# Transposing P in two row tiles of 64 queries, both heads in one step, into two PSUM banks

## The chip, the core and the metric

The kernel runs on one core of a Trainium2 chip. The metric is device time in microseconds (us) of one execution. Engines are named as in the profile: PE is TensorE (PEld its weight loads), DVE VectorE, ACT ScalarE, POOL GpSimd, SP the engine that issues most DMAs.

## The reference, cut to what is computed

```python
def _attn_ref(q, k, v, w1, b1, w2):          # B, H, S, D = 2, 8, 576, 64
    scores = scale * np.matmul(q, k.transpose(0, 1, 3, 2))
    ...
    x = (psi_rel / psi_i)[..., None]
    h = np.maximum(x @ w1 + b1, 0.0)
    bias = h @ w2
    scores = scores + bias.transpose(2, 0, 1)[None, :, :, :]
    scores = scores - np.max(scores, axis=-1, keepdims=True)
    attn = np.exp(scores)
    attn = attn / (np.sum(attn, axis=-1, keepdims=True) + 1e-09)
    return np.matmul(attn, v).astype(np.float32)
...
    x = np.ascontiguousarray(attn_out.transpose(0, 2, 1, 3)).reshape(B * S, H * D)
    x = _moe_ref(x=x, **moe_kwargs)
    return _moe2_ref(x=x, **moe2_kwargs)
```

Attention over 576 positions with a small learned bias for each pair of positions; then a mixture of four experts and a second feed-forward layer, both plain matrix products with elementwise work between them. Only the attention part is touched.

## The kernel before, in words

The attention part comes first and takes about the first 194 us of the span; the two feed-forward parts follow and are not touched. Attention works on pairs of heads: `n` = 0 to 7 is a batch and a head pair, and each `n` has nine score tiles (`g` = 9n to 9n+8): four chunks `c` of 128 queries for each of the two heads `h`, and a last tile (`c` = 4) with the remaining 64 queries of both heads side by side.

For each score tile the work runs like this. `scores` (L670) multiplies q by k into a PSUM tile `big`; `biased` (L684, DVE) adds the bias and finds the row maximum; `exps` (L692, ACT) writes the exponentials P and their sums; `norm_add`, `norm_recip` (L697, L702, DVE) and `norm` (L712, POOL or DVE) divide. Then P, which has queries on its partitions, must be turned so that keys lie on the partitions: `transp` (L729) turns four blocks of 128 x 128 of one head into one PSUM bank, and `transp_rest` (L742, L745) the 64 keys of each head that are left over. In each such instruction the weights that PE loads are a block of P and what streams through is the unit matrix `ident`. `copies` (L755 on ACT, L757 on DVE) brings the turned blocks from PSUM to the tiles `pt` and `pe`. When half of the queries of `n` are there, `av` (L770) multiplies them by v, and ACT and DVE write the result as `x` (L781, L785). `qk_T` (L627) turns q and k of the next `n`; its weights are 128 x 128 blocks too, with a unit matrix of type fp32r streaming.

PSUM has eight banks here: four for the tag `one`, which `transp`, `transp_rest`, `qk_T` and `av` share, and two tiles `big` of two banks each for the scores.

PE runs in different shapes: `scores`, `transp` and `qk_T` use the full array (128 rows, 128 columns), `av` two column tiles of 64 columns, and the bias products (L479) four column tiles of 32. The order of all instructions in attention is made when the program is built: `schedule` gives each step a duration, an urgency (from the numbers in `CFG`) and the steps it waits for, and `Flow.emit` picks from those that are ready; a change of PE's shape costs the time in `TURN` there, and tables in `PICK` say which engine takes a step. The numbers in `CFG` are the same before and after.

Of the kernel before, what the change touches and what calls it, by code (L numbers as in the profile page):

```python
# [18 lines left out]
B, H, S, D, HID = 2, 8, 576, 64, 32  # L19
# [5 lines left out]
P = 128  # L25
# [3 lines left out]
def f32_of_bits(b):  # L29
# [15 lines left out]
START = dict(PE=6.0, ACT=5.06, DVE=5.06, POOL=6.0, SP=7.5)  # L45
ARRIVES = dict(k=7.5, q=8.5, ident=6.5, ltab=10.0)
PORT = {("DVE", "hid"), ("DVE", "norm"), ("DVE", "low")}
TURN = {(32, 128): .22, (32, 64): .15, (64, 128): .16, (64, 32): .15, (128, 32): .11, (128, 64): .14}
NAMES = dict(D="DVE", A="ACT", P="POOL")
PICK = dict(hid="DDAAAADDDADDDDDDAADDDDDDDDAADDDDDDADDADADADDADADADADAADDDDDDDAADDADAADDD"  # L50
              "AADDADADADADDADDADAAADADDDDDAADADDDADADDDDDAADDAADDADAADDDADDDADDDDDAADD",
# [2 lines left out]
            copy="AADDADDAAADAAADADDDADAAADAADADDAAADDDDADAADDDAAAADAAAAAADAAADDAADDDAADAA",  # L54
            rest="AAAAAAAAAAAAAAAADDAAAAAAADAAAAAAAADDAAAAAAADDAAADAAADAAAAAAAAADAAADAAADA",
            high="PPPAAPPAPPAAAPPP",
            low="PPPPDPPDPDDPPDPP")

LAG = {"PE": .2, "ACT": .16, "DVE": .17, "POOL": .14, "SP": 1.5, "": 0.0, "own": .1, "ownPE": 0.0}
# [18 lines left out]
class Flow:  # L78
# [24 lines left out]
    def earliest(self, o):  # L103
        t = max(self.free[o["eng"]], o["after"])
        if o["port"]:
            t = max(t, self.free["port"])
        for h in o["take"]:
            users = self.caps[h["set"]]
            if len(users) > users[0]:
                end = users[-users[0]]["end"]  # L110
                if end is None:
                    return None
                t = max(t, end + LAG["own"])
        return t
# [58 lines left out]
class Kernel:  # L173
# [470 lines left out]
    def attention(self):  # L644

        nc, early = self.nc, self.early
# [57 lines left out]
        def norm(g, e):  # L704
            n, c, h = where(g)
            eng = nc.vector if e == "DVE" else nc.gpsimd
            ri = rsums[n, c][:, h:h + 1]
            pt = Pt[n, c]
            sl = slice(S * h, S * h + S)
            if c == 4:  # L710
                eng.tensor_scalar(out=pt[:, S:S + 64], in0=pt[:, 512:S], scalar1=ri, scalar2=1.0, op0=ALU.mult, op1=ALU.mult)
            eng.tensor_scalar(out=pt[:, sl], in0=pt[:, sl], scalar1=ri, scalar2=1.0, op0=ALU.mult, op1=ALU.mult)  # L712

        def pt_tiles(n, half):
            if (n, half) not in PT:
                W = (256, 320)[half]
                PT[n, half] = (self.att.tile([P, 4, 2, W], F32, tag=f"pt{half}", bufs=2, name="pt"),
                               self.att.tile([P, W], F32, tag=f"pe{half}", bufs=2, name="pe"))
            return PT[n, half]

        def transp(g):

            n, c, h = where(g)
            main, _ = pt_tiles(n, 0 if c < 2 else 1)
            pt = Pt[n, c]
            o = P * (c % 2) if c < 4 else 256
            ps = self.one().rearrange("p (e i) -> p e i", e=4)
            for e in range(4):
                nc.tensor.transpose(ps[:, e, :], pt[:, 640 * h + e * P:640 * h + e * P + P], self.ident)  # L729
            if c < 4:  # L730
                todo = [(ps, main[:, :, h, o:o + P])]
            else:
                todo = [(ps.rearrange("p e (h q) -> p e h q", h=2), main[:, :, :, 256:320])]
            parts[g] = (todo, [])

        def transp_rest(g):
            n, c, h = where(g)
            _, shared = pt_tiles(n, 0 if c < 2 else 1)
            ps = self.one()
            if c < 4:  # L740
                for i in range(2):
                    nc.tensor.transpose(ps[:, P * i:P * i + P], Pt.pop((n, c - 1 + i))[:, 512:640], self.ident)  # L742
                rest = [(ps[:, 0:256], shared[:, 0:256])]
            else:
                nc.tensor.transpose(ps[:, 0:P], Pt.pop((n, c))[:, 512:640], self.ident)  # L745
                rs = [slice(64 * hh, 64 * hh + 64) for hh in range(2)]
                rest = [(ps[r, r], shared[r, 256:320]) for r in rs]
            parts[g] = (parts[g][0], rest)

        parts = {}  # L750

# [49 lines left out]
        def schedule():  # L801

            def off(kind, n):

                return cfg[kind][min(n, 2) + (n == 7)]

            fl = Flow(cfg["EPS"], cfg["M"], self.behind, **START)
            Top, Sop, Rop, Lop, Lop2, split_op, qk_ops, stk = ({} for _ in range(8))
            biasop = {}
            last_store, made = self.bias_ops(fl, biasop)  # L810
            identr = fl.op("", ARRIVES["ident"], 0, lambda: None)
# [37 lines left out]
            for n in range(8):  # L849
                p_hold = {}  # L850
                for r in range(9):
                    g = 9 * n + r
                    c, h = r // 2, r % 2
                    half = 0 if c < 2 else 1
                    big = fl.hold("big", 2)
                    last = r == 8
                    Sop[g] = fl.op("PE", 1.2 if last else .58, g + off("S", n), lambda g=g: scores(g), qk_ops[n, "k"] + qk_ops[n, "q"] + [biasop[n // 2, c]],
                                   take=[big], free=[stk[n, "k"], stk[n, "q"]] if last else [])
                    ph = fl.hold("P", NPB) if h == 0 else ph
                    Rop[g] = fl.op("DVE", .71, g + off("R", n), lambda g=g: biased(g), [Sop[g], biasop.get((n // 2, c)), Rop[g - 1] if h else None], take=[ph] if h == 0 else [], free=[big])  # L860
# [6 lines left out]
                    for g in ([g] if last else [g - 1, g]):  # L867
                        h = (g - 9 * n) % 2
                        no = fl.pick("norm", g, {"POOL": .88 if last else .72, "DVE": .6 if last else .42}, g + off("N", n), lambda e, g=g: norm(g, e), [ao])
                        one, one2 = fl.hold("one", 4), fl.hold("one", 4)  # L870
                        rest = last or h and c % 2
                        take = [one]
                        if (n, half) not in pt_hold:
                            pt_hold[n, half] = fl.hold("PT", 4)
                            take.append(pt_hold[n, half])
                        to = Top[g] = fl.op("PE", .44, g + off("T", n), lambda g=g: transp(g), [no, Top.get(g - 1)], take=take)
                        Lop[g] = fl.pick("copy", g, {"ACT": .5, "DVE": .6}, g + off("H", n), lambda e, g=g: copies(g, 0, e), [to], free=[one])
                        if h and not rest:
                            ph_even = ph
                        if rest:  # L880
                            to = fl.op("PE", .09 if last else .19, g + off("T", n) + .1, lambda g=g: transp_rest(g), [to], take=[one2],
                                       free=[ph] if last else [ph_even, ph])
                            Lop2[g] = fl.pick("rest", g, {"ACT": .44 if last else .3, "DVE": .3 if last else .33}, g + off("H", n) + .1, lambda e, g=g: copies(g, 1, e), [to], free=[one2])
                    if n % 2 and (h == 1 or last) and n < 7:
                        biasop[n // 2 + 1, c] = fl.op("SP", 1.6 if last else .45, g + off("b", n), lambda n=n, c=c: self.load_bias(n // 2 + 1, c), [Rop[g], last_store if last else None], pipe=.9 if last else 1.85)
                    if r in (3, 8):
                        gs = range(9 * n, 9 * n + 4) if r == 3 else range(9 * n + 4, 9 * n + 9)
                        deps = [raw_op[n, "v"]] + [Lop[x] for x in gs] + [Lop2[x] for x in gs if x in Lop2]
# [452 lines left out]
```

## Time and profile before

| | before |
|---|---|
| median of 3 runs | 784.37 us (784.01 to 786.3) |
| the profiled execution | 784.95 us |
| its span in the profile | 783.2 us |
| PE busy in the span | 764.3 us (98%) |
| DVE, ACT, POOL busy | 638.4, 462.3, 373.1 us |

The span is the profiled part of one execution; 1.8 us lie around it. Busy times of PE include the pipeline's overlap, so a busy PE is not one at its best pace. The chain of work that ended last, which the rows below use, lists pieces that follow one another without a gap: the time of a piece is what it added to the chain.

### The profile page before, as it was taken

How to read it: one execution, taken by the hardware profiler on the slowest of the kernel's cores; microseconds unless marked ns; L12 is line 12 of the kernel's file. 1: busy time of each engine (PE TensorE's matmuls, PEld its weight loads, DVE VectorE, ACT ScalarE, POOL GpSimd, SP SyncE). 2: the span in 40 equal slices, each digit the busy share in tenths (PEclk: the TensorE clock that was granted, in tenths of full speed). 3: DMA queues.
4: the chain of work that ended last, by engine and by line, in shares of the span. 5: the costliest groups of instructions: out<-in, count | busy, mean ns of one | idle time of the engine just before them, and what ended most of it. 6: DMA issues, size and time to landing. Idle time of an engine off the chain costs nothing.

```text
span 783.2 us, 13021 instructions
## 1 busy us (share of the span) xinstructions
PE 764.3 (98%) x4756; PEld 657.3 (84%) x4756; DVE 638.4 (82%) x1139; ACT 462.3 (59%) x892; POOL 373.1 (48%) x361
## 2 busy tenths in 40 slices
PE   6889999999999999999999999999999999999997
PEld 3338888876989989889989889989888989999996
DVE  7998989874788888788888788887679877887775
ACT  7997898783434333333333333333279998887772
POOL 1123544260285553465453365453257777755442
PEclk9999999999999999999999999999999999999999
DMA  6898885730024433444333444332221311000012
GB/s 179 284 296 232 213 212 116 213 101 16 28 80 144 128 112 104 141 148 134 117 112 107 141 145 130 121 113 75 54 82 54 108 54 54 1 1 0 1 41 81
DMA packets 70448, 87.62 MB, mean 112 GB/s; under 512 B 34288, under 2 KB 42736, under 8 KB 70256
## 3 DMA queue, kind: packets, MB, share of 16 engines
q1 hardware_dynamic: 69808, 86.63, 37.1%
q8 instruction: 37, 0.61, 0.3%
q10 hardware_dynamic: 576, 0.16, 0.1%
q14 instruction: 27, 0.22, 0.1%
HBM read 60.15 MB, written 21.61 MB: 104 GB/s over the span
## 4 chain that ended last, share of the span: by engine, by line
PE 77%; DVE 6%; ACT 4%; issue 4%; DMA 4%; POOL 3%; SPq 1%; DVEq 0%; POOLq 0%; ACTq 0%
PE ps_o L945 21%; PE ps_o L1203 13%; PE ps_h L1195 12%; PE ps_y L1037 11%; PE ps_x L1037 8%; PE ps L670 3%; PE ps L770 3%; PE ps L729 3%; DMA rawq<-q 1%; DVE hid L464 1%; ACT P L692 1%; PE ps_x L935 1%; POOL we L344 1%; PE ps L479 1%; PE ps L627 1%
## 5 line engine op out<-in xcount | busy, mean ns | idle before, releaser
L945 PE MATMUL ps_o<-we,hs 128*128 128x512 f32 x810 | 203.4, 392 | 0.0
L945 PEld LDWEIGHTS ps_o<-we,hs 128*128 128x128 f32 x810 | 146.0, 188 | 25.9
L951 DVE SCALAR_TENSOR_TENSOR acc<-ps_o,prob,acc 128x512 f32<-128x512 f32 x135 | 99.8, 744 | 30.0 <-PE ps_o L945 29.9
L344 POOL TENSOR_TENSOR we<-wstg,we 128x512 fp32r<-128x512 f32 x39 | 55.8, 1450 | 129.6 <-ACT we L337 129.6
L1176 POOL TENSOR_TENSOR qq<-qq,ha 128x384 f32<-128x384 f32 x48 | 48.9, 1020 | 74.4 <-ACT qq L1173 70.8
L1203 PE MATMUL ps_o<-wmh,hs 128*128 128x512 f32 x252 | 83.4, 391 | 0.0
L1195 PE MATMUL ps_h<-x,wmh 128*128 128x384 f32 x288 | 73.7, 336 | 0.0
L975 ACT ACTIVATE hs<-ps_x 128x576 fp32r<-128x576 f32 x32 | 20.9, 652 | 80.9 <-DVE ps_x L1049 74.2
L692 ACT ACTIVATE P<-P,nm 128x576 f32<-128x576 f32 x72 | 55.6, 781 | 6.2 <-DVE nm L684 3.9
L684 DVE CUSTOM_DVE_ANT_0 P<-ps,bias 128x576 f32<-128x576 f32 x72 | 53.4, 750 | 6.4 <-PE ps L670 2.7
L712 POOL TENSOR_SCALAR P<-P,ri 128x576 f32<-128x576 f32 x42 | 33.6, 809 | 47.4 <-DVE ri L702 26.8
L1203 PEld LDWEIGHTS ps_o<-wmh,hs 128*128 128x128 f32 x252 | 47.3, 188 | 9.8 <-POOL hs L1187 0.4
L1195 PEld LDWEIGHTS ps_h<-x,wmh 128*128 128x128 f32 x288 | 52.6, 188 | 2.0
L370 POOL TENSOR_TENSOR wu<-wt,wu 128x512 fp32r<-128x512 f32 x28 | 36.2, 1315 | 36.4 <-ACT wu L366 36.4
L1187 POOL TENSOR_TENSOR hs<-pp,hs 128x384 fp32r<-128x384 f32 x48 | 51.8, 1079 | 3.2 <-issue 2.8
L479 PE MATMUL ps<-hid,wm 128*32 128x288 f32 (+17 forms) x352 | 41.0, 495 | 9.8 <-DVE hid L464 6.1
L1182 DVE SCALAR_TENSOR_TENSOR qq<-qq,rr 128x384 f32<-128x384 f32 x48 | 26.6, 553 | 29.3 <-ACT rr L1181 28.2
L670 PE MATMUL ps<-kh,qs 128*128 128x288 f32 x168 | 49.7, 318 | 0.1
L1203 PE MATMUL ps_o<-wml,hs 128*128 128x512 f32 x126 | 49.5, 393 | 0.0
L1037 PEld LDWEIGHTS ps_x<-sums,wu 128*128 128x128 f32 x336 | 47.5, 188 | 2.2
L1037 PEld LDWEIGHTS ps_y<-x,wu 128*128 128x128 f32 x336 | 47.5, 188 | 2.2
L1037 PEld LDWEIGHTS ps_y<-sums,wu 128*128 128x128 f32 x336 | 47.5, 188 | 2.2
(146 smaller groups left out, 1871.1 us busy)
## 6 DMA issues: line engine op xcount, KB each, us to landing
wstg<-moe_w SPq DMA_DIRECT2D x32, 512.0 KB, 3.9
bias_d<-bo SPq DMA_DIRECT2D x32, 295.5 KB, 3.6
bias<-bias_d SPq DMA_DIRECT2D x16, 576.0 KB, 5.2
w<-moe_w_in SPq DMA_DIRECT2D x16, 512.0 KB, 4.2
w<-moe_w_out SPq DMA_DIRECT2D x16, 512.0 KB, 3.8
kl<-kh SPq DMA_DIRECT2D x16, 288.0 KB, 4.7
w_u<-wmag SPq DMA_DIRECT2D x16, 256.0 KB, 2.5
w_d<-wmag SPq DMA_DIRECT2D x16, 256.0 KB, 2.4
```

The costliest lines, as they stand in the source:

```text
L344: eng.tensor_tensor(out=lo[:, sl], in0=stg[:, sl], in1=hi[:, sl].bitcast(F32), op=ALU.subtract)
L479: nc.tensor.matmul(to[32 * q:32 * q + 32, 0:b - a], lhsT=wm, rhs=hs[q][:, a:b], start=True, stop=True)
L670: nc.tensor.matmul(ps[:, half, dst:dst + w], lhsT=lhs, rhs=k[:, src:src + w], start=(i == 0), stop=(i == len(m) - 1))
L684: nc.vector.tensor_tensor_reduce(out=Pt[u][:, S * h:S * h + S].rearrange("p (a b) -> p a b", a=2), in0=ps[:, :, 0:288], in1=self.bias_t[n ...
L692: nc.scalar.activation(out=pt, in_=pt, func=AF.Exp, scale=-1.0, bias=stat.pop(g), accum_out=sums[n, c][:, h:h + 1])
L945: nc.tensor.matmul(ps, lhsT=a, rhs=w[:, f, :], start=(f == i == 0), stop=(f == 1 and i == 2))
L951: nc.vector.scalar_tensor_tensor(out=acc[:, t], in0=ps, scalar=pr, in1=acc[:, t], op0=ALU.mult, op1=ALU.add)
L1037: nc.tensor.matmul(ps[:, half, 0:288], lhsT=wu[:, w, i, k], rhs=x[v][:, k, 288 * half:288 * half + 288], start=(start and k == j == 0), st ...
L1176: nc.gpsimd.tensor_tensor(out=qq, in0=qq, in1=ha, op=ALU.mult)
L1187: nc.gpsimd.tensor_tensor(out=lo, in0=pp, in1=hi.bitcast(F32), op=ALU.subtract)
L1195: nc.tensor.matmul(ps, lhsT=w[:, k, fo:fo + P], rhs=x2_rows(q, v, k), start=(k == i == 0), stop=(k == 3 and i == 2))
L1203: nc.tensor.matmul(ps, lhsT=a[:, P * tt:P * tt + P], rhs=w[:, f % 2, :], start=(f == i == 0), stop=(f == 3 and i == 2))
```

## The change

One step now turns both heads' blocks of a chunk of 128 queries. The 128 x 128 block is split by queries: rows 0 to 63 and rows 64 to 127 of P are each loaded as weights of 64 rows and 128 columns into their own half of the array's rows, 64 columns of the unit matrix stream through each, and each half writes to its own bank of the tag `one`. The step takes two such banks at once, and waits for both heads' `norm`. The rest of two chunks, and the last tile with its rest, are split in the same way. The planner gets durations for the new steps, a shape of PE of its own (`ROWS`), times for turning to it and from it, and two short tables for the added copies. Where 328 blocks were turned by 328 matmuls, there are now 656.

```diff
+ROWS = 65
+TURNED = dict(T=.5, last=.35, rest=.14)
-TURN = {(32, 128): .22, (32, 64): .15, (64, 128): .16, (64, 32): .15, (128, 32): .11, (128, 64): .14}
+TURN = {(128, 65): .15, (65, 128): .2, (65, 32): .15, (32, 65): .2, (64, 65): .15, (65, 64): .15, (32, 128): .22, (32, 64): .15, (64, 128): .16, (64, 32): .15, (128, 32): .11, (128, 64): .14}
...
+        def halves(at, src, *tiles):
+            for r, ps in enumerate(tiles):
+                rows = slice(64 * r, 64 * r + 64)
+                nc.tensor.transpose(ps[:, 64 * at:64 * at + 64], src[rows], self.ident[rows, rows])
+
         def transp(g):
...
-            ps = self.one().rearrange("p (e i) -> p e i", e=4)
+            ps = self.one(), self.one()
+            if c < 4:
+                for e in range(4):
+                    for h in range(2):
+                        halves(2 * e + h, pt[:, 640 * h + e * P:640 * h + e * P + P], *ps)
+                o = P * (c % 2)
+                parts[g] = [[(ps[r].rearrange("p (x i) -> p x i", x=8), main.rearrange("p e h i -> p (e h) i")[:, :, o + 64 * r:o + 64 * r + 64])] for r in range(2)]
+                return
             for e in range(4):
-                nc.tensor.transpose(ps[:, e, :], pt[:, 640 * h + e * P:640 * h + e * P + P], self.ident)
...
+                halves(e, pt[:, e * P:e * P + P], *ps)
+            halves(4, Pt.pop((n, c))[:, 512:640], *ps)
...
-                to = Top[g] = fl.op("PE", .44, g + off("T", n), lambda g=g: transp(g), [no, Top.get(g - 1)], take=take)
...
+                    take = ones = [fl.hold("one", 4) for _ in range(2)]
...
+                    to = Top[g] = fl.op("PE", TURNED["last" if last else "T"], g + off("T", n), lambda g=g: transp(g), norms + [Top.get(g - 1)], take=take, free=[ph] if last else [], mode=(ROWS, ROWS))
```

Two places in PE's order show how the change moves instructions. In these rows `ps<-ident,P` is a turning of P, `ps<-kh,qs` and `ps<-kl,qs` are scores, `ps<-pt,rawv` and `ps<-pe,rawv` are `av`; the numbers are the output's partitions and columns. The first place is late in attention, behind an `av`. Before, four steps of turning (one head's chunk each), one score tile and the rest of two chunks stood like this:

```order
L729 MATMUL ps<-ident,P 128x128 x16
L670 MATMUL ps<-kh,qs 128x288
L670 MATMUL ps<-kl,qs 128x288
L670 MATMUL ps<-kh,qs 128x288
L670 MATMUL ps<-kl,qs 128x288
L742 MATMUL ps<-ident,P 128x128 x2
```

After the change, at the same place, one step of turning (both heads of a chunk) stands between the `av` and the scores:

```order
L779 MATMUL ps<-pe,rawv 64x256 x2
L730 MATMUL ps<-ident,P 128x64 x16
L676 MATMUL ps<-kh,qs 128x288
L676 MATMUL ps<-kl,qs 128x288
```

A run of turnings between score tiles is now a change of PE's shape on either side, where before it was none. The second place is the end of attention. Before, all turnings of the last `n` were done, then three `av` in a row, then the first product of the feed-forward part (`ps<-x,we`, 24 matmuls):

```order
L729 MATMUL ps<-ident,P 128x128 x16
L742 MATMUL ps<-ident,P 128x128 x2
L729 MATMUL ps<-ident,P 128x128 x4
L745 MATMUL ps<-ident,P 128x128
L770 MATMUL ps<-pt,rawv 64x320 x8
L770 MATMUL ps<-pe,rawv 64x320 x2
L770 MATMUL ps<-pt,rawv 64x256 x8
L770 MATMUL ps<-pe,rawv 64x256 x2
```

After the change that product is cut in three pieces, which stand between four runs of turnings, ahead of the last `av`:

```order
L730 MATMUL ps<-ident,P 128x64 x16
L945 MATMUL ps<-x,we 128x288 x6
L730 MATMUL ps<-ident,P 128x64 x16
L945 MATMUL ps<-x,we 128x288 x15
L730 MATMUL ps<-ident,P 128x64 x4
L945 MATMUL ps<-x,we 128x288 x3
L730 MATMUL ps<-ident,P 128x64 x10
L779 MATMUL ps<-pt,rawv 64x320 x8
L779 MATMUL ps<-pe,rawv 64x320 x2
L945 MATMUL ps_x<-x,we 128x288 x24
```

What moved: the product no longer stands behind the last `av`, and each of its pieces is entered from a run of row tiles. Counted over the whole attention part, PE's order before enters the full array 19 times, two column tiles 10 times and four column tiles 9 times; after the change it enters the full array 46 times, row tiles 40 times, two column tiles 15 times and four 9 times.

## Rows read from the trace of the kernel before

**Rows 1.** Busy time in three stretches; in brackets the instructions.

```profile
core 0: us, PE busy (x) PEld busy (x) DVE busy (x) ACT busy (x) POOL busy (x), PEclk, DMA share, GB/s
0.00:60.00 60.00, 48.58 (x405) 22.17 (x409) 54.31 (x145) 54.26 (x113) 10.67 (x19) 1.00 0.82 255
60.00:194.00 134.00, 132.37 (x1088) 108.25 (x1079) 109.58 (x311) 103.78 (x253) 54.84 (x72) 1.00 0.61 158
194.00:783.00 589.00, 583.34 (x3273) 526.90 (x3271) 474.53 (x685) 304.29 (x527) 307.57 (x270) 1.00 0.28 87
```

**Rows 2.** PE's waits behind 195 us: total us, times, longest.

```profile
PE ps_o L945 <- DVE acc L949: 0.6, 1, 0.6
PE ps_x L1229 <- DVE acc L951: 0.5, 1, 0.5
PE ps_x L1229 <- DVE pp L1184: 0.2, 1, 0.2
```

**Rows 3.** The chain that ended last, 128 to 200 us: start, us, what.

```profile
128.90 0.87 PE ps L729 x8
...
178.01 5.00 PE ps L770 x40
183.01 1.90 PE ps L729 x16
184.90 0.22 PE ps L742 x2
...
193.36 3.37 PE ps L935 x24
196.73 3.18 PE ps_x L935 x24
```

**Rows 4.** PE's groups of turnings: count, busy us, mean ns, idle before.

```profile
L729 PE MATMUL ps<-ident,P 128*128 128x128 f32 x288 | 39.9, 276 | 1.2 <-DVE x L785 0.7 <-DVE P L712 0.2
...
L742 PE MATMUL ps<-ident,P 128*128 128x128 f32 x32 | 6.2, 275 | 0.0
...
L745 PE MATMUL ps<-ident,P 128*128 128x128 f32 x8 | 2.2, 276 | 0.0
```

**Rows 5.** The chain again, 94 to 99 us.

```profile
94.23 0.47 PE ps L627 x6
94.69 0.46 PE ps L729 x4
...
98.86 0.47 PE ps L627 x6
```

**Rows 6.** Groups of weight loads, 0 to 200 us: count, busy us, mean ns, idle before.

```profile
L729 PEld LDWEIGHTS ps<-ident,P 128*128 128x128 f32 x288 | 31.8, 141 | 6.6 <-issue 2.0 <-POOL P L712 1.8 <-PE ps L770 1.0
...
L479 PEld LDWEIGHTS ps<-hid,wm 128*32 128x32 f32 x352 | 14.7, 113 | 30.4 <-ACT hid L462 8.0 <-DVE hid L464 6.4 <-POOL wm L443 5.8
L627 PEld LDWEIGHTS ps<-identr,splk 128*128 128x128 f32 x72 | 7.5, 140 | 3.9 <-POOL splk L611 1.8 <-PE ps L479 0.8 <-ACT hid L462 0.6
```

**Rows 7.** DVE's groups of copies and divisions, 0 to 200 us.

```profile
L757 DVE COPY pt<-ps 128x512 f32<-128x512 f32 x30 | 20.0, 683 | 3.0 <-PE ps L729 2.6 <-DMA bias<-bias_d 0.4
L712 DVE TENSOR_SCALAR P<-P,ri 128x576 f32<-128x576 f32 x30 | 17.3, 594 | 0.2
...
L757 DVE COPY pe<-ps 128x256 f32<-128x256 f32 x8 | 3.3, 418 | 0.1
...
L757 DVE COPY pe<-ps 64x64 f32<-64x64 f32 x8 | 1.7, 216 | 0.1
```

**Rows 8.** ACT's groups of copies, 0 to 200 us.

```profile
L755 ACT ACTIVATE pt<-ps 128x512 f32<-128x512 f32 x42 | 23.9, 598 | 3.4 <-PE ps L729 3.3
...
L755 ACT ACTIVATE pe<-ps 128x256 f32<-128x256 f32 x8 | 3.1, 386 | 1.3 <-PE ps L742 1.3
...
L755 ACT ACTIVATE pe<-ps 64x64 f32<-64x64 f32 x8 | 1.7, 216 | 0.0
```

**Rows 9.** POOL's division, 0 to 200 us.

```profile
L712 POOL TENSOR_SCALAR P<-P,ri 128x576 f32<-128x576 f32 x42 | 33.6, 809 | 47.4 <-DVE ri L702 26.8 <-DVE sm L697 6.3 <-ACT kh L635 4.0
```

More of the change, by code (lines that the diff above doesn't have):

```diff
@@ L56 @@
             high="PPPAAPPAPPAAAPPP",
+            copyb="DADADADA",
+            restb="AAAAAAAAAAAAAAAA",
             low="PPPPDPPDPDDPPDPP")
@@ L106, in earliest @@
             t = max(t, self.free["port"])
+        asked = {}
         for h in o["take"]:
-            users = self.caps[h["set"]]
-            if len(users) > users[0]:
-                end = users[-users[0]]["end"]
+            users, k = self.caps[h["set"]], asked.get(h["set"], 0)
+            asked[h["set"]] = k + 1
+            if len(users) + k > users[0]:
+                end = users[k - users[0]]["end"]
                 if end is None:
@@ L719, in pt_tiles @@
             return PT[n, half]
+        def halves(at, src, *tiles):
+            for r, ps in enumerate(tiles):
+                rows = slice(64 * r, 64 * r + 64)
+                nc.tensor.transpose(ps[:, 64 * at:64 * at + 64], src[rows], self.ident[rows, rows])
         def transp(g):
             n, c, h = where(g)
-            main, _ = pt_tiles(n, 0 if c < 2 else 1)
+            main, shared = pt_tiles(n, 0 if c < 2 else 1)
             pt = Pt[n, c]
-            o = P * (c % 2) if c < 4 else 256
-            ps = self.one().rearrange("p (e i) -> p e i", e=4)
-            for e in range(4):
-                nc.tensor.transpose(ps[:, e, :], pt[:, 640 * h + e * P:640 * h + e * P + P], self.ident)
[L730 to L734, printed above, removed]
+            ps = self.one(), self.one()
[6 more added lines that the diff above has]
+                return
+            for e in range(4):
+                halves(e, pt[:, e * P:e * P + P], *ps)
+            halves(4, Pt.pop((n, c))[:, 512:640], *ps)
+            parts[g] = [[(ps[r][:, 0:256].rearrange("p (e i) -> p e i", e=4), main[:, :, r, 256:320]),
+                         (ps[r][64 * r:64 * r + 64, 256:320], shared[64 * r:64 * r + 64, 256:320])] for r in range(2)]
         def transp_rest(g):
@@ L738, in transp_rest @@
             _, shared = pt_tiles(n, 0 if c < 2 else 1)
[L739 to L748, printed above, removed]
+            ps = self.one(), self.one()
+            for i in range(2):
+                halves(i, Pt.pop((n, c - 1 + i))[:, 512:640], *ps)
+            parts[g] += [[(ps[r][:, 0:P].rearrange("p (c i) -> p c i", c=2), shared[:, 0:256].rearrange("p (c r i) -> p c r i", c=2, r=2)[:, :, r])] for r in range(2)]
         parts = {}
@@ L807, in schedule @@
             fl = Flow(cfg["EPS"], cfg["M"], self.behind, **START)
-            Top, Sop, Rop, Lop, Lop2, split_op, qk_ops, stk = ({} for _ in range(8))
+            Top, Sop, Rop, Lop, split_op, qk_ops, stk = ({} for _ in range(7))
             biasop = {}
@@ L866, in schedule @@
                     ao = fl.op("DVE", .11, g + off("A", n), lambda g=g: norm_recip(g), [ao])
[L867 to L875, printed above, removed]
-                        to = Top[g] = fl.op("PE", .44, g + off("T", n), lambda g=g: transp(g), [no, Top.get(g - 1)], take=take)
[L877 to L883, printed above, removed]
@@ new lines, in schedule @@
+                    norms = []
+                    for x in ([g] if last else [g - 1, g]):
+                        norms.append(fl.pick("norm", x, {"POOL": .88 if last else .72, "DVE": .6 if last else .42}, g + off("N", n), lambda e, x=x: norm(x, e), [ao]))
+                    rest = not last and c % 2
+                    take = ones = [fl.hold("one", 4) for _ in range(2)]
+                    if (n, half) not in pt_hold:
+                        pt_hold[n, half] = fl.hold("PT", 4)
+                        take = take + [pt_hold[n, half]]
@@ new lines, in schedule @@
+                    to = Top[g] = fl.op("PE", TURNED["last" if last else "T"], g + off("T", n), lambda g=g: transp(g), norms + [Top.get(g - 1)], take=take, free=[ph] if last else [], mode=(ROWS, ROWS))
+                    Lop[g] = [fl.pick("copyb" if last and r else "copy", n if last and r else g - 1 + r if not last else g, {"ACT": .7, "DVE": .6} if last else {"ACT": .5, "DVE": .6}, g + off("H", n),
+                                      lambda e, g=g, r=r: copies(g, r, e), [to], free=[ones[r]]) for r in range(2)]
@@ new lines, in schedule @@
+                    if c % 2 == 0:
+                        ph_even = ph
+                    if rest:
+                        ones = [fl.hold("one", 4) for _ in range(2)]
+                        to = fl.op("PE", TURNED["rest"], g + off("T", n) + .1, lambda g=g: transp_rest(g), [to], take=ones, free=[ph_even, ph], mode=(ROWS, ROWS))
+                        Lop[g] += [fl.pick("restb" if r else "rest", 2 * n + c // 2 if r else g, {"ACT": .27, "DVE": .25}, g + off("H", n) + .1,
+                                           lambda e, g=g, r=r: copies(g, 2 + r, e), [to], free=[ones[r]]) for r in range(2)]
@@ L887, in schedule @@
                         gs = range(9 * n, 9 * n + 4) if r == 3 else range(9 * n + 4, 9 * n + 9)
-                        deps = [raw_op[n, "v"]] + [Lop[x] for x in gs] + [Lop2[x] for x in gs if x in Lop2]
+                        deps = [raw_op[n, "v"]] + [y for x in gs if x in Lop for y in Lop[x]]
                         one = fl.hold("one", 4)
```

## The prediction, made blind

> **What bounds the kernel now.** I read the busy times by stretch first. From 60 to 194 us, the second part of attention, PE is busy 132.37 of 134 us, DVE 109.58 and ACT 103.78 [rows 1]. In the first 60 us PE is busy 48.58, DVE and ACT 54.31 and 54.26: that stretch is not PE's. Behind 194 us PE is busy again, 583.34 of 589 us, and the list of its waits there has three lines that come to 1.3 us [rows 2]: what attention gains or loses moves the rest by as much. So the question is what the change does to PE between 60 and 194 us, and the chain of waits shows that stretch as PE pieces that follow one another [rows 3]. The granted clock is 1.00 in all three stretches, so no term below is a clock's.
>
> **The price of a turned block now.** Eight blocks behind other full-array work add 0.87 us to the chain, 0.109 each [rows 3]. The 288 of L729, the 32 of L742 and the 8 of L745 are 328 blocks [rows 4]: 328 x 0.109 = 35.8 us of PE time.
>
> **The price after the change.** No row shows row tiles. A block becomes two loads of 64 rows by 128 columns and two streams of 64 columns. Three bounds:
>
> - If the halves run side by side and every load is hidden, only the stream counts, and it is half as long: 0.109 / 2 = 0.0545 a block, 17.9 us in all, 17.9 less than now.
> - If the loads set the pace: `qk_T` loads 128 x 128 weights as well, its loads last 140 ns against 141 for P [rows 6], and six of them add 0.47 us, 0.078 each [rows 5]. Its stream is of type fp32r and quicker than P's, so what holds it at 0.078 is, I take it, the load; with P's stream cut to 0.0545 the load would be the longer one here too. With the loads of the two halves side by side a block takes 0.078: 25.6 us, 10.2 less.
> - If the loads of the two halves go one behind the other, it takes 2 x 0.078 = 0.156: 51.2 us, 15.4 more.
>
> Do loads of different tiles go side by side? Those of the bias products do: 352 loads of 113 ns are 39.8 us, within 14.7 us of busy time [rows 6], 2.7 at a time. These are column tiles with 32 columns each; I take the same for row tiles, and 0.078, since the load keeps its 128 columns and `qk_T` is the nearest row: **-10.2 us**.
>
> **The changes of shape.** This is the part that the diff doesn't show and the order does. Sixteen blocks behind an `av` add 1.90 us [rows 3], 0.156 more than 16 x 0.109: the price of going from column tiles to the full array for a turning. The first product, 24 matmuls behind an `av`, takes 3.37 us against 3.18 for the next 24 [rows 3]: 0.19. PE now enters row tiles 40 times where it never did (40 x 0.156 = 6.2), enters the full array 46 times for 19 (27 x 0.19 = 5.1), and column tiles of 64 fifteen times for ten (5 x 0.156, an estimate, = 0.8): **+12.1 us**. Before, the 70 borders in that order between turnings and scores or `qk_T` were within one shape and cost next to nothing (four blocks behind `qk_T` take 0.46 us, 0.02 over 4 x 0.109 [rows 5]). Row tiles could be entered for less than column tiles: the lower bound is nothing, and that ends at -10.2; the upper one is that of the rows, as I know of none that is dearer. The Trainium skill says, in "TensorEngine Tiling (Array Packing)", Key Properties, that changing the tiling mode, not just the tile, drains the engine. The rows show the price for column tiles; no row shows it for row tiles. Without that rule this term would be nothing and the sum about 9 us better; with it, it stands.
>
> **The copies.** A copy of eight blocks of 64 columns is as long as one of four of 128: 128x512, 0.683 us on DVE, 0.598 on ACT [rows 7, 8]. The last tile's copy is cut in two of 128x256 (like 0.418 and 0.386), and the rest's 16 copies of 128x256 become 32 of 128x128, which lie between the 64x64 (0.216) and the 128x256; I take 0.3. By the order DVE now has 23 long copies for 30 and ACT 37 for 42, with 7 and 9 of 128x256 and 8 and 24 of 128x128 in exchange. DVE: -7 x 0.683 + 7 x 0.418 + 8 x 0.3 - 8 x 0.418 = -2.8 us; ACT: -5 x 0.598 + 9 x 0.386 + 24 x 0.3 - 8 x 0.386 = +4.6 us. ACT has 30 us free in the 134, so this costs nothing by itself; without that cover it would be the 4.6.
>
> **New waits.** A step of turning now waits for both heads' division, where the first head's blocks could go ahead by themselves; a division is 0.594 us on DVE and 0.809 on POOL [rows 7, 9]. And it takes two of the four banks `one` at once, for which `qk_T` and `av` stand too. Behind a waiting turning on PE stand scores, for which DVE waits, and `av`, for which ACT waits. Now the loads of L729 sit idle 6.6 us in all [rows 6]; I bound the new waits between nothing (the planner has 40 runs to fill around) and as much again, 6.6, and take **+1.5**. The move of the first product ahead of the last `av` costs its three entries, counted above; behind the last `av` PE goes on with a product that needs no x of this `n`, so it is not missed as a cover.
>
> **Sum.** -10.2 + 12.1 + 1.5 = +3.4 us. The profiled execution took 784.95 us, 1.8 more than its span, so 788.35; it lies 0.58 above the median of the runs shown, which makes 787.8, and I say 788.
>
> **The rivals.** What 0.3% is here, 2.4 us, is about what a measurement of this kernel can tell from no change.
>
> 1. *The halves overlap fully (faster).* Then a block is 0.0545: -17.9 + 12.1 + 1.5 = -4.3, 780. For it: column tiles do run side by side. Against it: `qk_T` doesn't get below 0.078. It decides at a block of 0.0675 = 0.109 - 13.6 / 328; under 0.060 it is faster by more than 0.3%. The Trainium skill says in "TensorE: Matmul & The Clock Gate", Measured speedup vs the span model, that packed tiles take one matmul's duration and about 4 ns for each further tile. By that a pair would be an estimated 0.0585, -16.6 + 12.1 + 1.5 = -3.0, so 781; it is a figure for matmuls, and says nothing of the loads between them. Chance 0.22, with cheap entries counted in.
> 2. *In between (no change).* The diff's table books 0.5 us for a step of eight blocks, 0.0625 each; the old entry, 0.44 for four, is what the rows give (4 x 0.109). With 32 such steps, 8 last ones at 0.35 and 16 rests at 0.14 turning takes 21.0 us: -14.8 + 12.1 + 1.5 = -1.2, 783. It is a number that the planner plans by and no row. Chance 0.2.
> 3. *Loads one behind the other.* +15.4 + 12.1 + 1.5 = +29, 813. For it: the side-by-side rows are all of column tiles, and none has 128 columns. Chance 0.1.
> 4. *The waits.* Two banks at once starve the others, and the order, made by urgencies that are older than the new steps, leaves PE waiting 6.6 us more instead of 1.5: 793. For it: only four banks, and DVE and ACT busy for 80% of the stretch. Chance 0.13.
>
> **How the numbers follow.** The forecast has 0.35. Its own range goes from 785 (no new wait, a pair at 0.073) to 791. Faster: rival 1 and a little of 2, 0.24. Same: most of 2 and the lower end of the forecast, 0.25. Slower: the rest, 0.51. The range goes from 780, rival 1's time, to 797, which holds rival 4 with some more, and leaves out rival 3 and the better half of 1, about 2 in 10.
>
> **What would show it.** In the changed profile: a run of 16 halves that adds 0.6 to 0.65 us to the chain, with 0.16 on top when it comes from another shape (0.44 means rival 1, 1.25 rival 3); scores behind it that take 0.19 more; the stretch from 60 us to the first product of the feed-forward part longer by some 3 us, with PE still busy in nearly all of it; PE's idle time before turnings near 8 us and not 13. The prediction is wrong if turning into row tiles costs clearly less than 0.15, if a pair takes under 0.065, or if the first 60 us move.

## The result, and the profile after

| | before | after |
|---|---|---|
| median, taken side by side | 785.29 us (784.01 to 786.3) | 790.41 us (790.25 to 790.86) |
| the profiled execution | 784.95 us | 790.39 us |
| its span | 783.2 us | 788.6 us |

The ratio is 1.0067, with an interval from 1.0048 to 1.0086: the change made the kernel slower by about 5 us. The forecast was 788 in a range of 780 to 797, with a chance of 0.51 for slower. What the sum was made of came out quite differently, though, and the profile shows it.

I read the same views in the same order. Busy time in the three stretches of [rows 1], columns as there, of the kernel after:

```profile
0.00:60.00 60.00, 48.66 (x434) 21.84 (x438) 54.57 (x146) 54.77 (x116) 10.65 (x19) 1.00 0.82 256
60.00:194.00 134.00, 128.57 (x1337) 99.45 (x1329) 106.46 (x310) 102.96 (x264) 55.34 (x72) 0.97 0.61 158
194.00:783.00 589.00, 587.29 (x3318) 529.80 (x3317) 474.07 (x685) 306.72 (x535) 307.45 (x270) 1.00 0.27 86
```

In the middle stretch PE is idle for 134 - 128.57 = 5.43 us, where [rows 1] left 134 - 132.37 = 1.63. And the granted clock, 1.00 before, is 0.97 there. Neither stood in my sum in that size. The first stretch is as it was.

The groups of turnings, which answer to [rows 4] and the first row of [rows 6] (count, busy us, mean ns, idle before):

```profile
L730 PE MATMUL ps<-ident,P 64*128 64x64 f32 x656 | 32.1, 232 | 1.2 <-ACT pt L764 0.3 <-ACT pe L764 0.2 <-POOL P L718 0.2
...
L730 PEld LDWEIGHTS ps<-ident,P 64*128 64x128 f32 x656 | 25.3, 140 | 11.3 <-issue 4.7 <-ACT pt L764 1.1 <-DVE P L718 0.8
```

Twice as many loads of the same length (140 ns for 141) are busy for less time than before, 25.3 us for 31.8 of L729 alone. The 656 of 140 ns are 91.8 us, 3.6 at a time; the 288 of 141 ns were 40.6 us, 1.3 at a time.

The chain of waits, from the first `av` behind 60 us to the first products of the feed-forward part (start, us, what); it answers to [rows 3] and [rows 5]:

```profile
60.65 2.36 PE ps L779 x20
...
72.32 8.79 DMA kl<-kh
...
85.10 0.64 PE ps L730 x16
85.74 0.73 PE ps L676 x4
...
87.24 0.60 ACT pt L764
...
88.75 0.77 ACT kh L641 x2
89.51 0.78 ACT qs L641 x2
...
91.15 1.26 PE ps L676 x4
...
92.81 1.26 PE ps L676 x4
...
94.80 2.22 PE ps L676 x8
...
192.53 0.64 PE ps L730 x16
...
198.37 0.38 ACT pt L764
...
198.79 3.28 PE ps L779 x20
202.07 2.98 PE ps_x L945 x21
```

And three rows of the same view of the kernel before, for the comparison:

```profile
61.28 2.31 PE ps L770 x20
...
73.09 0.53 PE ps L670 x4
...
80.76 6.39 DMA rawq<-q
```

Three things are to be seen here. First, a run of 16 halves (eight blocks) takes 0.64 us, entry included. By the ends of its matmuls the two halves of a block end 2 to 7 ns apart, the first block adds 0.206 us and each of the seven others 0.062, so a block is **0.062 us** and the entry 0.206 - 0.062 = 0.144; the four scores behind it take 0.73 where they took 0.53, so the way back is 0.20. (The expectations below still reckon with 0.0586 a block and 0.174 an entry, from the mean of the fifteen steps between the sixteen ends, 29.3 ns. Eight of these steps lie within a block and only seven between blocks, so twice the mean is too little for a block and leaves too much for the entry; the run as a whole is the same.) Secondly, the chain leaves PE, for a transfer of `kl` and for copies on ACT. That alone shows no wait: the chain of the kernel before leaves it too, for a transfer of `rawq`, while PE is busy with other work. Thirdly, from 90.8 us on four scores take 1.26 us and eight 2.22.

What PE did wait for is in the list of its waits from 55 to 203 us (total us, times, longest; the four longest of eight, the others come to 0.9 us):

```profile
PE ps L676 <- DVE nm L690: 1.8, 3, 1.0
PE ps L633 <- POOL splq L617: 1.3, 1, 1.3
PE ps L676 <- DMA kl<-kh: 1.2, 1, 1.2
PE ps L779 <- ACT pt L764: 0.5, 1, 0.5
```

And why scores became slow is in the clock's column of the stretches (us, PE busy, granted clock, DMA share, GB/s):

```profile
78.00:80.00 2.00, 1.56 (x11) 1.00 1.06 261
80.00:82.00 2.00, 0.85 (x6) 1.00 1.05 340
...
90.00:91.00 1.00, 0.89 (x16) 0.89 0.37 83
91.00:92.00 1.00, 1.00 (x7) 0.50 1.23 212
...
96.00:97.00 1.00, 1.00 (x7) 0.50 0.70 161
97.00:98.00 1.00, 1.00 (x9) 0.70 0.61 136
```

From 90.8 to 97.6 us the chip granted 0.50, the lower of its two levels (1.2 instead of 2.4 GHz). The same stretch of the kernel before:

```profile
78.00:80.00 2.00, 2.00 (x18) 1.00 1.02 232
80.00:82.00 2.00, 2.00 (x18) 1.00 1.05 376
```

So PE had waited ahead of the fall, 1.59 of the 4 us from 78 to 82. But the fall came 9 us behind that; from 82 to 87 us PE was busy throughout, and from 87 to 91 us for 3.64 of 4 us. Which of these waits the fall belongs to, this trace doesn't show.

**Where the 5.4 us went.** From that first `av` to the second product, the kernel before took 196.73 - 61.28 = 135.45 us and the one after 202.07 - 60.65 = 141.42: +5.97. The start lies 0.63 earlier, the rest is unchanged to 0.1. I added up, matmul by matmul, what each end adds to the one ahead of it, and set what is above the usual pace of its kind apart: the work of PE fell from 129.3 to 126.6 us (-2.6), its waits rose from 6.2 to 11.8 (+5.6), 4.9 of it before 100 us, and the slow clock cost +3.0. The total is measured; how it splits is an estimate, as it rests on what I took as the usual pace. (The waits in this count are larger than idle time in the table, since the modelled ends of matmuls cover part of them.) So the row tiles did bring time, and waits and the clock took more.

### The profile page after: what moved, and what is told of

The parts are those of the page before. It is cut to its first block, busy times and chain, and to the rows that moved or that the text cites. A ratio compares the mean times of both kernels' runs of the same rounds, so it can differ in the third digit from the quotient of the medians.

```text
span 788.6 us, 13657 instructions
## 1 busy us (share of the span) xinstructions
PE 765.7 (97%) x5084; PEld 651.7 (83%) x5084; DVE 637.0 (81%) x1142; ACT 464.5 (59%) x913; POOL 373.4 (47%) x361
## 4 chain that ended last, share of the span: by engine, by line
PE 78%; DVE 6%; DMA 4%; issue 4%; ACT 3%; POOL 3%; SPq 1%; DVEq 0%; POOLq 0%; ACTq 0%
PE ps_o L955 20%; PE ps_o L1213 12%; PE ps_h L1205 12%; PE ps_y L1047 10%; PE ps_x L1047 8%; PE ps L779 4%; PE ps L676 4%; PE ps L730 2%; DVE hid L470 1%; PE ps_x L945 1%; POOL we L350 1%; DMA kl<-kh 1%; DVE P L690 1%; PE ps L485 1%; PE ps_y L945 1%
## 5 line engine op out<-in xcount | busy, mean ns | idle before, releaser
L485 PE MATMUL ps<-hid,wm 128*32 128x288 f32 (+18 forms) x352 | 41.0, 492 | 9.5 <-DVE hid L470 6.1
```

What stands on the lines that cost most here:

```text
L485: nc.tensor.matmul(to[32 * q:32 * q + 32, 0:b - a], lhsT=wm, rhs=hs[q][:, a:b], start=True, stop=True)
```

## The experiments

Why are there new waits and a slow clock? The step could cost them by itself: it needs both heads' rows and two of four banks. Or it lies in the order: all of attention is set by one list of priorities, and a step with another duration shuffles all that follows. These two stand together as theory A at first; theory B is that the row tiles pull the clock down. Experiments 4 to 8 then tell the two halves of A apart, as theories S (structure) and O (order).

**1. The order of after, without row tiles.** Each block is turned by one matmul on the full array again, head by head into the same two banks; the planner still reckons with row tiles and gives the same order.

```diff
-                for e in range(4):
-                    for h in range(2):
-                        halves(2 * e + h, pt[:, 640 * h + e * P:640 * h + e * P + P], *ps)
+                for h in range(2):
+                    for e in range(4):
+                        nc.tensor.transpose(ps[h][:, P * e:P * e + P], pt[:, 640 * h + e * P:640 * h + e * P + P], self.ident)
```

> The changed kernel with its own order of instructions, but each pair of 64-row halves is one 128 x 128 turning on the full array again (328 matmuls, the same two banks a step). Theory A (the change's PE work is a gain of about 2.6 us; what it loses are new waits of PE that come from the order, +5.6, and a fall of the granted clock after them, +3.0): turning costs 328 x (0.109 - 0.0586) = 16.5 us more and the changes of shape fall away (-13.1), so up to 3.4 us slower than the changed kernel where PE is the limit and nothing where it waits: 790 to 794 us, waits between 60 and 100 us as before, clock at 0.5 again for some us near 90. Theory B (row tiles themselves pull the clock down): clock 1.00 throughout, 787 to 790 us.

Measured: 790.59 us (787.46 to 793.6), 1.0047 (1.0024 to 1.0069) of before. Its rows of the middle stretch and of some microseconds in it, columns as above:

```profile
60.00:194.00 134.00, 128.22 (x1032) 103.60 (x1026) 106.42 (x309) 102.70 (x262) 55.57 (x72) 0.99 0.61 158
```

```profile
81.00:82.00 1.00, 0.00 (x0) 1.00 1.02 336
82.00:83.00 1.00, 0.34 (x3) 1.00 1.09 358
...
84.00:85.00 1.00, 1.00 (x6) 0.50 1.05 321
```

No row tile is left, and yet PE is idle for 5.78 us and the clock falls, right behind idle time. So row tiles are not needed for the clock to fall, and theory B does not hold as the explanation. Whether they make a fall likelier is not shown; all four executions of the changed kernel have a mean clock of 0.995. Here not every execution has the fall: five of the ten, with a mean clock of 0.999 to 1.000, took 787.5 to 789.9 us, and the five with 0.994 to 0.998, the profiled one among them, 791.3 to 793.6. That distance of some 4 us is not the clock's alone: the profiled one has a single fall, of 3.4 us at 0.50, which can cost PE 1.7 us at most. What else differs between the two groups is not shown. The unchanged kernel has such executions as well: beside this run it took 787.29 and 787.37 us at 0.996, and 783.63 to 786.3 at 0.999 to 1.000.

**2. Both heads and two banks on the full array, planned as such.** As in 1, with the planner told so:

```diff
-TURNED = dict(T=.5, last=.35, rest=.14)
+TURNED = dict(T=.88, last=.55, rest=.22)
...
-                    to = Top[g] = fl.op("PE", TURNED["last" if last else "T"], g + off("T", n), lambda g=g: transp(g), norms + [Top.get(g - 1)], take=take, free=[ph] if last else [], mode=(ROWS, ROWS))
+                    to = Top[g] = fl.op("PE", TURNED["last" if last else "T"], g + off("T", n), lambda g=g: transp(g), norms + [Top.get(g - 1)], take=take, free=[ph] if last else [], mode=(128, 128))
```

> The other part of the change alone: both heads in one step with two banks, full-array turning, and the planner told its true durations (0.88, 0.55, 0.22 us) and no change of shape. Theory A (waits come from steps that are twice as long and hold two banks, put in order by urgencies made for the old steps): slower than before without any row tile, 788 to 797 us, with PE's waits between 60 and 194 us of 10 us or more against 6.2. Theory B (the loss is of row tiles: shapes and clock): no slower than before, 784 to 787 us.

Measured: 791.92 us (791.33 to 792.84), 1.0076 (1.0061 to 1.0091), at a clock of 1.000. Its middle stretch:

```profile
60.00:194.00 134.00, 128.19 (x1036) 103.74 (x1028) 105.25 (x307) 101.63 (x260) 54.33 (x72) 1.00 0.62 158
```

PE's idle time there is 134 - 128.19 = 5.81 us. (The 10 us or more of waits that theory A named are in another count, by the ends of the matmuls, which I did not make here.) So with no row tile and no slow clock it is slower than before by some 6 us. That leaves the step's structure or the order.

**3. PE kept busy.** In the changed kernel, of the turning of q and k at `n` = 3 two parts of three are done three times over, so that PE has more to do where it waited.

```diff
-            nc.tensor.transpose(ps[:, P * i:P * i + P], spl[:, c].rearrange("p a d -> p (a d)"), self.identr)
+            for _ in range(3 if n == 3 and part else 1):
+                nc.tensor.transpose(ps[:, P * i:P * i + P], spl[:, c].rearrange("p a d -> p (a d)"), self.identr)
```

> The changed kernel, with twelve of the turnings of q and k of n = 3 done three times over (24 more matmuls of 0.085 us, 2.0 us, that write the same values), in the stretch from 87 to 91 us where PE waits for ACT's copies just before the granted clock falls. Theory A (the fall follows a stretch in which PE has little to do): the clock stays at 1.00, and the time is 3.0 us less and up to 2.0 more than the changed kernel's: 787.4 to 789.4 us. Theory B (row tiles pull the clock down): it falls as before, 790.4 to 792.5 us.

Measured: 791.68 us (789.75 to 793.29), 1.0071 (1.0046 to 1.0095). The clock fell all the same, now from 81.6 to 85.0 us, behind two microseconds in which PE was busy for 0.07 and 0.09. The added work had not filled this gap; the expectation of a clock of 1.00 failed, and the trial settles nothing about the waits.

**4 and 5. The kernel before, in another order.** Nothing of the work is touched; the planner only reckons with another duration for a turning step.

```diff
-                        to = Top[g] = fl.op("PE", .44, g + off("T", n), lambda g=g: transp(g), [no, Top.get(g - 1)], take=take)
+                        to = Top[g] = fl.op("PE", .43, g + off("T", n), lambda g=g: transp(g), [no, Top.get(g - 1)], take=take)
```

> The kernel before, with one number of its planner altered: a turning step of four blocks is put down at .43 us in place of .44. Every instruction stays, with its shape, its banks and its data; only the order that the planner writes out becomes another. Theory O (the order before was one that its priorities had been tuned to, and any change of the steps' costs loses that, so that the change's +5 us lie in the order and not in the row tiles or the two banks): 4 to 9 us slower than before, 789 to 795, with new waits of TensorE before 100 us. Theory S (the structure costs it: a turning step that waits for both heads' rows and takes two banks): no structure is altered here, so within 0.3% of before, 783.5 to 788.5.

> The same with .46 in place of .44: a second order of the same instructions. Theory O: again 4 to 9 us slower than before, 789 to 795, at other waits than with .43. Theory S: within 0.3% of before, 783.5 to 788.5.

Measured: 794.6 us (792.98 to 794.84), 1.0115 (1.0089 to 1.0141) with .43, and 790.9 (789.76 to 793.03), 1.0079 (1.0057 to 1.0101) with .46. Here is the middle stretch with .43, and the list of PE's waits from 55 to 203 us:

```profile
60.00:194.00 134.00, 127.27 (x1030) 104.05 (x1030) 107.17 (x301) 102.26 (x246) 54.61 (x72) 0.99 0.61 158
```

```profile
PE ps L729 <- DVE P L712: 3.8, 2, 2.2
PE ps L670 <- DVE nm L684: 2.6, 2, 1.8
PE ps L479 <- DVE nm L684: 2.4, 1, 2.4
```

With .46 the stretch is:

```profile
60.00:194.00 134.00, 128.41 (x1048) 104.98 (x1039) 107.67 (x307) 101.08 (x248) 55.14 (x72) 1.00 0.60 157
```

Idle time is 6.73 us with .43 and 134 - 128.41 = 5.59 with .46, for 1.63 before. The same instructions, with the same banks and one head at a time, lose as much as the change did, or more. In the trace with .43 the clock falls too, twice for 3.4 us, and up to 3.4 of its 9 us are the clock's; in that with .46 it stays at 1.00. Theory S said nothing would move; it falls as the cause of such waits in general. The order before sits on numbers that fit it, and a hundredth of a microsecond in a planned duration is enough to lose that.

**6 and 7. The change in an order fitted to it.** The changed kernel with other numbers in `CFG` and `PICK`, looked for until the planner's own reckoning of PE's end was back where it stands for the kernel before (its reckoning only chose the candidate; the time is the chip's). One dependence is written out, which the order after happened to keep: the rest of two chunks is turned behind the first chunk's step.

```diff
-            high="PPPAAPPAPPAAAPPP",
+            high='PPPAAPPPPPAPAAPP',
...
-            low="PPPPDPPDPDDPPDPP")
+            low='PPPDDPPDDPPPDDPP')
...
-                        to = fl.op("PE", TURNED["rest"], g + off("T", n) + .1, lambda g=g: transp_rest(g), [to], take=ones, free=[ph_even, ph], mode=(ROWS, ROWS))
+                        to = fl.op("PE", TURNED["rest"], g + off("T", n) + .1, lambda g=g: transp_rest(g), [to, Top[g - 2]], take=ones, free=[ph_even, ph], mode=(ROWS, ROWS))
```

The second kernel of the pair has this order to the letter, and the full array as in 1.

> The changed kernel, with its two row tiles, both heads in one step and two banks, and with other numbers in the two tables that set the order and the engine of each small piece of work (the priorities of each kind of step by head, and which of two engines takes each copy, division and split). Theory O: TensorE's new waits of 5.6 us go again and its 2.6 us less of work stay, so 2 to 5 us below before: 781 to 785. Theory S: the waits come from the step that needs both heads and two banks, so another order helps little: 788 to 792, as the changed kernel. If the clock falls to 0.5 for some us again, up to 3 us come on top with either.

> The order of after_retuned to the letter, but every block turned by one matmul on the full array, 128 x 128, into the same two banks: no row tile is left. By the pace of the changed kernel's turnings (328 blocks, 0.0586 us in place of 0.109: 16.5 us less, against 13.1 us of new entries between shapes) TensorE has about 3.4 us more work than in after_retuned. If the row tiles are a gain by themselves: 2 to 4 us slower than after_retuned. If the entries eat the gain: within 1.5 us of it.

Measured: 781.06 us (779.15 to 782.46), 0.9943 (0.9921 to 0.9966) with row tiles, and 784.0 (782.94 to 785.02), 0.9984 (0.9974 to 0.9993) with the full array, on the same chip, before at 785.22. The middle stretch and two waits of the first, and some of its chain:

```profile
60.00:194.00 134.00, 132.40 (x1417) 103.42 (x1418) 113.46 (x327) 104.92 (x269) 50.72 (x65) 1.00 0.61 157
```

```profile
PE ps L617 <- POOL splq L601: 0.8, 1, 0.8
PE ps L617 <- DVE pt L750: 0.3, 1, 0.3
```

```profile
139.24 0.64 PE ps L714 x16
...
163.56 0.72 PE ps L660 x4
...
166.29 0.46 PE ps L714 x10
```

The chain of the full-array kernel:

```profile
178.16 0.53 PE ps L660 x4
178.69 0.87 PE ps L726 x8
```

Idle time is back at 1.60 us (1.62 in the full-array kernel), and the row tiles are worth 784.0 - 781.06 = **2.9 us** in the same order, one fitted to the tiles: their net effect alone. That lies in the 2 to 4 that the blocks and the entries give. The two profiled executions, both at a clock of 1.000, lie 783.79 - 779.15 = 4.6 us apart, and two of the five executions with row tiles have a mean clock of 0.997; so 3 to 5 us is as far as this goes. This kernel is faster than both of the case, by 4.2 us than before: theory O. Of the 4.2 us, 785.22 - 784.0 = 1.2 come without any row tile. The kernel before was not fitted anew beside it, so what another search would have given there stays open.

**8. A second fitted order.** Another set of numbers for the changed kernel, found apart from the first.

> The changed kernel with a second set of numbers in the two tables, found apart from the first. Theory O (the change costs time only where the order was not fitted to it): below before again, 781 to 785, with TensorE's waits between 60 and 200 us under 3 us. If after_retuned was a lucky order and the steps of two heads and two banks cost waits in general: 786 to 791.

Measured: 784.12 us (782.47 to 786.34), 0.9972 (0.9957 to 0.9987). Below before again (786.22 on this chip, which is another one than in 6 and 7; so it is in 9 to 11), with one wait of 2.1 us for `splq`:

```profile
60.00:194.00 134.00, 130.88 (x1416) 101.30 (x1405) 113.52 (x329) 100.89 (x259) 55.73 (x72) 1.00 0.60 157
```

That is 134 - 130.88 = 3.12 us of idle time, just over the 3 that I had named. The first order was a good one, but not the only one.

**9. The halves apart.** As `after_retuned`, but each step turns all halves of one row tile and then all of the other.

```diff
-                for e in range(4):
-                    for h in range(2):
-                        halves(2 * e + h, pt[:, 640 * h + e * P:640 * h + e * P + P], *ps)
+                for r in range(2):
+                    for e in range(4):
+                        for h in range(2):
+                            half(2 * e + h, pt[:, 640 * h + e * P:640 * h + e * P + P], r, ps[r])
```

> after_retuned with the same halves in another sequence: in each turning step first all halves of the one row tile, then all of the other, so that a half's neighbours stand in its own row tile. Same count, same shapes, same two banks, same entries. Theory P (a block costs 0.0586 us because its two halves, neighbours in different row tiles, run side by side): without such neighbours a half costs its own stream, 0.109 / 2 = 0.0545, a block 0.109 again, a run of 16 halves adds some 0.95 us in place of 0.64, and the kernel is about 328 x 0.050 = 16 us slower than after_retuned, 794 to 799 beside 781. Theory H (a half is cheap by itself, because its load and stream are short): 0.0293 us a half in any sequence, within 1.5 us of after_retuned.

Measured: 787.37 us (786.3 to 788.54), 1.0015 (1.0001 to 1.0028). The chain has:

```profile
122.26 0.27 PE ps L713 x4
...
144.55 0.94 PE ps L713 x16
```

A run of 16 takes 0.94 us, as theory P said, where the halves by turns took 0.64; theory H falls. The whole is 7.9 us slower (profiled executions, 787.03 against 779.15), half of the 16 that I expected; by the medians, taken on two chips, it is 6.3. In the trace of one such run the halves of one row tile end 62 or 63 ns apart, but PE starts the second tile's while the first tile's last three are still going, so three of eight pairs run side by side even so. In all thirteen runs of 16 between 60 and 200 us the matmul that closes the first tile, eighth in the program, ends eleventh. Each row tile is a stream of its own at 62 ns a half. That is also the pace of a whole block by turns, so there the second half adds next to nothing. I had expected 54.5 ns a half and had reckoned without TensorE reaching ahead: 0.144 + 13 x 0.062 = 0.95 for the run, by another sum than theory P's.

**10 and 11. Every block turned twice.** `after_retuned` with each half done twice (`for r, ps in 2 * [*enumerate(tiles)]`), and its full-array partner with each block done twice.

> after_retuned with each half turned twice into the same place, always one half of each row tile by turns: 328 blocks of turning more, no entry more. What it adds is a block's price where TensorE is the bound: by the pace in the trace 328 x 0.0586 = 19.2 us, 800 beside 781; by the 0.078 that the prediction took for the loads 25.6 us, 807. Copies start later by a run's length, which may cost some 2 us in waits with either.

> retuned_full with each block turned twice into the same place on the full array: 328 blocks more. By the pace of before 328 x 0.109 = 35.8 us, 820 beside 784. With twice_rows this gives what a block costs in either form without the entries; the difference of the two should be 328 x 0.050 = 16.5 us by the trace's pace and 10.2 by the prediction's 0.078.

Measured: 796.13 us (795.85 to 796.28), 1.0118 (1.01 to 1.0136), and 816.62 (816.1 to 818.61), 1.0384 (1.0361 to 1.0406). The profiled executions lie 796.28 - 779.15 = 17.1 and 816.94 - 783.79 = 33.2 us above their partners. By the count of the trace before, 18 of the 328 blocks are turned in the first 60 us, which are not PE's; on the other 310 that is 0.055 and 0.107 a block. By the pace in the traces, 0.062 and 0.109, it would be 19 and 34 us. With row tiles 2 us of the added work don't show in the time; PE's idle time in the middle stretch is down from 1.60 to 0.45 us:

```profile
60.00:194.00 134.00, 133.55 (x1883) 109.93 (x1875) 106.42 (x307) 104.31 (x260) 49.65 (x64) 1.00 0.61 157
```

By the medians the two lie 15.1 and 32.6 us above their partners, on another chip, on which before's median is 1.0 us higher. The prediction's 0.078 would have given 24, more than either count for the row tiles.

## Why the prediction was right, and where it was not

**What bounds the kernel**: right, by the busy time. The reading of [rows 3] as PE pieces that follow one another holds for the rows shown there only: of the chain of the kernel before from 60 to 196.7 us, over 50 us are other engines and transfers, with PE busy beside them. What attention lost between 60 and 200 us moved the end by as much, and experiments 10 and 11 show that PE work added there comes out in the time nearly in full.

**The block, 0.078 and -10.2 us**: this is the step that failed in size. It was 0.062, so 328 x (0.109 - 0.062) = 15.4 us less, and 14.6 on the 310 blocks that count. That loads of different row tiles go side by side was right. Wrong was "what holds it at 0.078 is, I take it, the load", carried over to loads of half the rows: a row tile takes a half with its load in 62 ns by itself. What holds `qk_T` at 0.078 no run shows. Rival 2's 0.0625, the number that the planner books, was nearest. Rival 1's second figure, from the Trainium skill's "TensorE: Matmul & The Clock Gate", Measured speedup vs the span model, is an estimate of 0.0585 for a pair: its about 4 ns for a further tile agree with the 2 to 7 ns between the ends of a pair's halves, and what I put too low in it was the first half, 54.5 ns where one alone takes 62.

**The changes of shape, +12.1 us**: right. Into row tiles 0.144 for my 0.156, back to scores 0.20 for 0.19; with my counts (40 x 0.144 + 27 x 0.20 + 5 x 0.156) +11.9. (Without this term my sum would have been 12.1 us better, 8.7 below before; the "about 9 us better" of the prediction is counted from before.) The Trainium skill's sentence in "TensorEngine Tiling (Array Packing)", Key Properties, that a change of the mode drains the engine, agrees; it gives no price, and the rows of column tiles did. Block and shapes together made PE's work 2.6 us less in the trace, where I had 1.9 more (-14.6 + 11.9 gives -2.7), and experiment 7 measured 2.9 us by the medians in another order.

**New waits, +1.5 us**: too small, +5.6. I had put them to the step, which needs two divisions and two banks. Experiments 4 to 7 show that orders which don't fit have such waits whatever the step looks like, and that fitted orders of this very step have far less of them (1.60 and 3.12 us of idle time, for 1.63 before and 5.43 after). Rival 4 had that ("made by urgencies that are older than the new steps") with 6.6 us and a chance of 0.13; it deserved more. What each single wait came from I did not take apart.

**The clock, not in the sum**: +3.0. "The granted clock is 1.00 in all three stretches, so no term below is a clock's" held for the profile of the kernel before only. In four of the five profiles in which I found a fall within attention (experiments 1, 3, 4 and 8) each fall came within 1 us behind a stretch of 2 us in which PE was busy for 0.16 to 0.41 us; in that of the changed kernel it came 9 us behind the longest waits. And not every such stretch is followed by one: the kernel before is busy for only 0.35 of the 2 us from 53 us on, the one with .46 for 0.17 of the 2 us from 95 us on, and the clock stays at 1.00. What decides between the two stays open, and so does how the change brought its fall about.

So -10.2 + 12.1 + 1.5 = +3.4 should have been about -14.6 + 11.9 + 5.6 + 3.0 - 0.6 for the earlier start = +5.3, against the 5.4 between the profiled executions. The forecast held because a gain that I had set too low stood against losses that I had set too low by more. That is luck: the sign of the result rests on the waits and the clock, of which my sum had 1.5 us of 8.6.

**What would show it**: the run of 16 halves (0.6 to 0.65) fits with 0.64, but that has the entry in it. Without it a run is 0.50, nearer to rival 1's 0.44, and a pair is under the 0.065 that I had named as proof against me: by that test this term was wrong. The scores behind (+0.19) and the first 60 us fit; the stretch from 60 us on grew by 5.97 us and not by 3; "PE still busy in nearly all of it" does not, and the idle time before turnings' loads is 11.3 us, between my 8 and the 13 of the waits.

## What to carry to other kernels

A kernel whose order comes from fitted numbers has to be refitted before a change to it is judged, and the old kernel with it: here two small changes of one planned duration cost 6 and 9 us, more than the change itself was worth in a fitted order (3 to 5 us). To tell the two apart, run the old work in a new order and the new order with the old work. Price an engine's pieces by their own stream and load in the new shape, and the borders between shapes apart: here 15.4 us of gain met 11.9 us of entries. And when pieces end in pairs, count from pair to pair: the mean over all ends gave a block too short.

## What the runs showed of the hardware that I had not expected

- Two row tiles of 64 rows are independent streams: 62 ns for a half with its load (64 x 128, fp32, 64 columns), the same 62 ns for two by turns, and overlap even where a series on one tile is followed by a series on the other; matmuls of the second tile then end ahead of earlier ones of the first (experiment 9).
- Into row tiles PE needs 0.144 us more, out of them to the full array 0.20, close to the prices of column tiles (0.156 and 0.19).
- Close behind some waits of PE, not behind all, the granted clock was 0.50, for 3.4 us at a time and for 6.8 in the changed kernel. Executions of one kernel, that of experiment 1, lay up to 6 us apart (787.46 to 793.6), the longer ones at the lower mean clock.
